# Storing a third of the decoded weights one block later, with a re-timed planner

## The chip, the cores and the metric

The kernel runs on one core of one Trainium2 chip. The metric is the device time of that core in microseconds, from one execution of the whole program. One profiled execution is read besides. Its engines are TensorE (PE, with its weight loads as PEld), VectorE (DVE), ScalarE (ACT), GpSimd (POOL) and SyncE (SP). Each takes its instructions in the order of the program.

## The reference

Attention with a distance bias, then two feed-forward networks (FFNs) on its output. All inputs are fp32 in value; the weights come to the device as 64-bit floats.

```python
B, H, S, D = 4, 8, 576, 64
scores = q @ k.T / sqrt(D)
cum    = cumsum(max(s, 0))
scores = where(causal, -1e9, scores + min(-(cum_i - cum_j), 0))
attn   = softmax(scores) @ v
x = attn reshaped to (2304, 512)
x = ((x @ w_a) * (x @ w_b)) @ w_out              # 512 -> 1536 -> 512
h = x @ w_in                                     # 512 -> 2048
g = max(h, 0) + alpha * min(h, 0)
out = g @ w_out2                                 # 2048 -> 512
```

## The kernel before

**Tiling.** The 2304 tokens are cut into five blocks, here called 1 to 5: four of 512 and one of 256. A block's FFN runs over 12 tiles of 128 hidden features of the first network and 16 of the second. Each product of fp32 numbers is three matmuls of halves that TensorE takes at full rate (fp32r): each factor is split into a high part, the value rounded, and a low part, the rest. `mm3` (L1078 to L1080) issues the three, with the weight's halves `wh` and `wl`; L1189 to L1191 do it for the last layer. A block takes 68 weights of 128x512 numbers (`NW`), and each feeds 4 x 3 = 12 matmuls.

**Where a weight comes from.** In block 1 it is loaded as 64-bit numbers (`raw<-in_w_dram`, 512 KB), then decoded to fp32: `top` on ACT (L987) and `w` on DVE (L278). `split` then makes `wh` on ACT (L270) and `wl` on DVE or POOL (L284). The decoded weight is also stored to a scratch tensor in DRAM, `w_d` (L1051, a DMA that ACT issues). In blocks 2 to 5 two decoded weights are loaded at a time (`raw<-w_d`, 512 KB) and only split. Six buffers hold split weights, five hold `raw`, and a handful hold `w32`, the decoded weight, which in block 1 comes free when the store has landed.

**Other work on the same engines.** In the first network `a_sb` is copied from a PSUM bank by ACT and `g` multiplied by DVE from the other bank; in the second, `m` (ACT, L262, then a scale on DVE, L289) and `g` (DVE). Each `g` is split into `gh` (ACT) and `gl` (DVE or POOL). PE can reuse a bank when its `g` is done. The attention of the next block is cut into steps that PE runs between the FFN's matmuls. Its bias tile `z` is made from `cb`, the cumulated sums broadcast over 128 rows by DMA (`cb<-cum_d`), on ACT (L575) or DVE; the softmax's sums and scales are on ACT, DVE and POOL (`z<-z,sm`, L289); `zt` transposes a tile on DVE, SP stores it (`zd<-zt`) and loads it back transposed (`pt<-zd`). `kh`, `kl` and `qs` are the split keys and queries.

**What sets the order.** The order of ACT, DVE, POOL and SP is made by a planner when the program is built. `Order` keeps open links of chains, each with its engines and an assumed duration; it takes the one that could start first by its own clock, and between equal starts the one due first, its ready time plus a slack (`SL_...`). That clock is pushed on by `run.pe(ns)` behind each piece of PE's work, with PE assumed at 2.4 GHz, and by `run.need(chain)` where PE's next instruction reads what the chain makes. `dma` (L293) gives a transfer's assumed rate and landing. `load_w` (L1006) holds the chains of one weight: loading, decoding, splitting, storing. Block by block the main loop (L1206 on) places the attention steps evenly between the FFN's pieces.

## Time and profile before

| | |
|---|---|
| median of three runs | 1001.83 us |
| the runs | 1000.83 to 1004.99 us |
| the profiled execution's own time | 1007.81 us |
| its span | 1006.0 us |
| busy in the span: PE, DVE, ACT, POOL | 982.2, 682.8, 553.5, 243.2 us |
| granted TensorE clock, mean | 0.993 |
| FFN of blocks 1 to 5 starts at | 56, 283.5, 499.8, 711.8, 904.7 us |

The span is what the trace covers; the time of that execution is 1.8 us longer. The page gives busy time of each engine, and the span in 40 slices of 25.15 us. Behind it the trace can be asked for stretches, for waits of an engine (what it lacked, and for how long), and for single instructions. A matmul's duration reaches beyond the start of the next one, so PE's pace is read from its starts.

### The profile page before, as it was taken

What the parts mean: (1) busy time and instruction counts of PE and PEld (TensorE: products, weight loads), DVE (VectorE), ACT (ScalarE), POOL (GpSimd) and SP (SyncE); (2) the same over time, 40 slices, a digit from 0 to 9 for tenths busy, and PEclk for the clock granted to TensorE, in tenths of its full rate; (3) what the DMA queues carried; (4) which work ended last, traced back from release to release, by engine and by line L of the source; (5) the groups of instructions that cost most, each with busy time, mean ns of one, the idle gap of its engine ahead of it and who ended that gap; (6) DMA issues with size and microseconds to landing.
All of it is one profiled execution on the core that took longest, in us unless ns stands there. A gap on an engine that the chain in (4) does not pass through costs nothing.

```text
span 1006.0 us, 16223 instructions
## 1 busy us (share of the span) xinstructions
PE 982.2 (98%) x5381; PEld 810.7 (81%) x5381; DVE 682.8 (68%) x1590; ACT 553.5 (55%) x1133; POOL 243.2 (24%) x307
## 2 busy tenths in 40 slices
PE   6999999998999999999999999999999999999998
PEld 5667777776888888788888888888888888889997
DVE  7887767885578676876468687964454465546685
ACT  5865656775565455654455446544433354446674
POOL 2121112321232233443132134422010032220032
PEclk9999999998999999999999999999999999999999
DMA  6599999999777758449287766554543424327551
GB/s 188 192 280 346 351 331 345 319 320 317 262 236 247 231 172 263 146 144 275 75 268 242 211 202 205 171 174 145 184 143 93 158 92 130 118 72 237 187 173 59
DMA packets 149156, 208.85 MB, mean 208 GB/s; under 512 B 36112, under 2 KB 80144, under 8 KB 149072
## 3 DMA queue, kind: packets, MB, share of 16 engines
q1 hardware_dynamic: 139280, 189.99, 59.2%
q10 hardware_dynamic: 9792, 17.83, 4.7%
q8 instruction: 42, 0.69, 0.3%
q14 instruction: 42, 0.34, 0.1%
HBM read 164.18 MB, written 43.59 MB: 207 GB/s over the span
## 4 chain that ended last, share of the span: by engine, by line
PE 86%; DMA 7%; DVE 3%; issue 1%; ACT 1%; POOL 1%; ACTq 0%; SPq 0%; POOLq 0%; DVEq 0%
PE bank L1078 20%; PE bank L1079 20%; PE bank L1080 19%; PE bank L1189 6%; PE bank L1190 6%; PE bank L1191 6%; PE bank L766 2%; DMA cb<-cum_d 2%; PE bank L502 2%; DMA raw<-in_w_dram 2%; PE bank L528 1%; PE bank L706 1%; DMA kq<-in_kq_b_dram 1%; PE bank L827 1%; DVE z L278 1%
## 5 line engine op out<-in xcount | busy, mean ns | idle before, releaser
L1078 PE MATMUL bank<-xh,wh 128*128 128x512 f32 (+1 forms) x800 | 299.1, 374 | 2.3 <-DVE g L278 2.3
L1079 PE MATMUL bank<-xl,wh 128*128 128x512 f32 (+1 forms) x800 | 295.1, 369 | 0.0
L1080 PE MATMUL bank<-xh,wl 128*128 128x512 f32 (+1 forms) x800 | 295.1, 369 | 0.0
L270 ACT ACTIVATE wh<-raw 128x512 fp32r<-128x512 f32 x268 | 167.3, 626 | 97.8 <-PE bank L1079 59.5
L284 DVE TENSOR_TENSOR wl<-raw,wh 128x512 fp32r<-128x512 f32 x188 | 131.3, 701 | 95.8 <-ACT wh L270 88.8
L284 POOL TENSOR_TENSOR wl<-raw,wh 128x512 fp32r<-128x512 f32 x84 | 111.0, 1322 | 335.8 <-ACT wh L270 292.4
L1078 PEld LDWEIGHTS bank<-xh,wh 128*128 128x128 f32 x800 | 151.0, 189 | 33.2 <-issue 4.1
L1080 PEld LDWEIGHTS bank<-xh,wl 128*128 128x128 f32 x800 | 151.0, 189 | 25.5
L1079 PEld LDWEIGHTS bank<-xl,wh 128*128 128x128 f32 x800 | 151.2, 189 | 25.0
L270 ACT ACTIVATE gh<-g 128x512 fp32r<-128x512 f32 (+1 forms) x140 | 82.3, 588 | 71.2 <-DVE g L278 68.2
L1189 PE MATMUL bank<-wh,gh 128*128 128x512 f32 x288 | 114.9, 399 | 4.6 <-ACT wh L270 4.6
L284 DVE TENSOR_TENSOR gl<-g,gh 128x512 fp32r<-128x512 f32 (+1 forms) x128 | 87.8, 686 | 43.6 <-ACT gh L270 41.9
L1190 PE MATMUL bank<-wl,gh 128*128 128x512 f32 x288 | 113.5, 394 | 0.0
L1191 PE MATMUL bank<-wh,gl 128*128 128x512 f32 x288 | 112.9, 392 | 0.0
L262 ACT ACTIVATE z<-z,mn 128x128 f32<-128x128 f32 (+4 forms) x144 | 82.9, 577 | 50.8 <-DVE mn L278 50.8
L1078 PE MATMUL bank<-gh,wh 128*128 128x512 f32 (+1 forms) x240 | 89.9, 374 | 1.1 <-ACT wh L270 1.1
L1079 PE MATMUL bank<-gl,wh 128*128 128x512 f32 (+1 forms) x240 | 88.7, 370 | 0.2 <-DVE gl L284 0.2
L1080 PE MATMUL bank<-gh,wl 128*128 128x512 f32 (+1 forms) x240 | 88.5, 369 | 0.0
L262 ACT ACTIVATE m<-bank 128x512 f32<-128x512 f32 (+1 forms) x80 | 44.2, 552 | 75.5 <-PE bank L1080 75.3
L289 DVE TENSOR_SCALAR m<-m,alpha_sb 128x512 f32<-128x512 f32 (+1 forms) x68 | 33.0, 486 | 59.6 <-ACT m L262 58.7
L1189 PEld LDWEIGHTS bank<-wh,gh 128*128 128x128 f32 x288 | 54.8, 190 | 17.6 <-ACT wh L270 5.0
L270 ACT ACTIVATE a_sb<-bank 128x512 f32<-128x512 f32 (+1 forms) x60 | 32.9, 548 | 62.1 <-PE bank L1080 58.3
(91 smaller groups left out, 1369.2 us busy)
## 6 DMA issues: line engine op xcount, KB each, us to landing
raw<-w_d SPq DMA_DIRECT2D x136, 512.0 KB, 4.2
raw<-in_w_dram SPq DMA_DIRECT2D x68, 512.0 KB, 6.0
w_d<-w ACTq DMA_DIRECT2D x68, 256.0 KB, 5.6
zd<-zt SPq DMA_DIRECT2D x48, 192.0 KB, 4.2
pt<-zd SPq DMA_DIRECT2D x48, 192.0 KB, 3.9
kq<-in_kq_a_dram SPq DMA_DIRECT2D x16, 512.0 KB, 5.7
vb<-in_v_dram SPq DMA_DIRECT2D x112, 64.0 KB, 4.0
zd<-zt SPq DMA_DIRECT2D x24, 256.0 KB, 2.2
```

Of the source, the lines that this page charges most:

```text
L262: nc.scalar.activation(o, i, func, **k)
L270: nc.scalar.activation(o, i, AF.Copy, scale=by)
L284: (nc.gpsimd if eng == "pool" else nc.vector).tensor_tensor(o, i0, i1, op=ALU.subtract)
L289: (nc.gpsimd if eng == "pool" else nc.vector).tensor_scalar(o, i, s0, s1, op0=ALU.mult, op1=ALU.mult)
L502: nc.tensor.matmul(d, qs[:, r * P:n], k[:, 0:n], start=i == 0, stop=i == 1)
L766: nc.tensor.matmul(pv[64 * j:64 * j + 64, r * P:(r + 1) * P], got[0][:, c, j * D:(j + 1) * D], p[:, :, r * (r + 1) // 2 + c, :], start=c = ...
L1078: nc.tensor.matmul(o, wh, ih, start=first, stop=False)
L1079: nc.tensor.matmul(o, wh, il, start=False, stop=False)
L1080: nc.tensor.matmul(o, wl, ih, start=False, stop=last)
L1189: nc.tensor.matmul(acc[t], gh[:, c], wh, start=first, stop=False)
L1190: nc.tensor.matmul(acc[t], gh[:, c], wl, start=False, stop=False)
L1191: nc.tensor.matmul(acc[t], gl[:, c], wh, start=False, stop=last)
```

## The change

**A third of the weights.** Pairs of weights with `i // 2 % 3 == 1`, 22 of 68, are not stored in block 1. In block 2 they are loaded as 64-bit numbers again, decoded in place (`w` lies in the first half of `raw`) and stored from there; `raw` comes free when that store has landed. From block 3 on all are loaded as pairs. So block 1 has 46 stores in place of 68 and block 2 has 22 in place of none; `raw<-in_w_dram` goes from 68 to 90, `raw<-w_d` from 136 to 125, `top` and `w` from 68 to 90 each.

**Planner's durations.** PE's matmuls get a gap of 13.3 ns and some attention steps a further 100 or 200 ns; transfers are assumed at 85 (170) bytes per ns, not 90 (180), and land 1500 ns, not 900, behind their end.

**Layer chains first.** The chains on which the FFN itself hangs (`copy_a`, `gate`, `rectify`, the split of `g`, the split of the first network's output) get a slack of -4000 ns, so they come before others that could start at the same time.

**Attention steps by what is ready.** A step whose scores, transposes or values are not ready by the planner's clock may be up to four steps late (`BEHIND`), and where PE would wait for a layer's chain, steps that are ready are placed there, up to four early (`EARLY`).

The core of the diff:

```diff
 BIG = 3.0e38
+GAP, SWITCH, LANDS = 13.3, 100, 1500
...
-SL_LOAD, SL_PARTS, SL_QK, SL_BIAS = 10000.0, 5000.0, 5000.0, 2500.0
+SL_LOAD, SL_PARTS, SL_QK, SL_BIAS, SL_FFN = 10000.0, 5000.0, 5000.0, 2500.0, -4000.0
...
-FASTER, BEFORE = 1.06, 6
+FASTER, BEFORE, BEHIND, EARLY = 1.06, 6, 4, 4
...
-        yield {"dma": prod(o.shape) / (180 if o.dtype == U16 else 90)}, 900
+        yield {"dma": prod(o.shape) / (170 if o.dtype == U16 else 85)}, LANDS
...
         i = n % NW
+        postponed = i // 2 % 3 == 1
+        new = n < NW or (n < 2 * NW and postponed)
+        kept = new and postponed == (n >= NW)
...
-            yield of_w32
-            w = wraw.tile([P, WN], I32, name="w32", tag="w32", bufs=W32)
...
+            if n < NW:
+                yield of_w32
+                w = wraw.tile([P, WN], I32, name="w32", tag="w32", bufs=W32)
...
+            else:
+                w = r[:, 0:WN]
             source.append(w)
             yield from decode(n, r, w)
-            run.give(of_raw, run.t)
+            if n < NW:
+                run.give(of_raw, run.t)
...
-            yield from split(f32(source[0]) if n < NW else source[0], h, l)
-            if n < NW:
+            yield from split(f32(source[0]) if new else source[0], h, l)
+            if kept:
                 run.spawn(keep(stored), run.t)
+            elif new:
+                run.give(of_w32, run.t)
...
-            run.give(of_w32, run.t)
+            run.give(of_w32 if n < NW else of_raw, run.t)
...
-        fetched = run.spawn(first() if n < NW else again(), slack=SL_LOAD)
-        stored = run.spawn(store()) if n < NW else None
+        fetched = run.spawn(first() if new else again(), slack=SL_LOAD)
+        stored = run.spawn(store()) if kept else None
...
-        run.pe(3 * o.shape[-1] / 2.4)
+        run.pe(3 * (o.shape[-1] / 2.4 + GAP))
...
+    def due():
+
+        while todo and want - (steps_in - len(todo)) > 0:
+            run.pump()
+            if want - (steps_in - len(todo)) < BEHIND and not possible(*todo[0]):
+                return
+            step()
+
+    def wait(*chains):
+
+        run.pump()
+        while not seen(*chains) and todo and possible(*todo[0]):
+            if steps_in - len(todo) - want >= EARLY:
+                break
+            step()
+            run.pump()
+        run.need(*chains)
...
-                used[0] = run.spawn(copy_a())
+                used[0] = run.spawn(copy_a(), slack=SL_FFN)
...
-                used[1] = run.spawn(gate(f))
+                used[1] = run.spawn(gate(f), slack=SL_FFN)
```

`possible` asks whether the chains that a step reads are done by the planner's clock; `take`, `into` and the layers call `wait` where they called `run.need`, and the same slack goes to `rectify`, `split_t` and `split_by`.

**What it moves.** All of PE's instructions are the same, and in the same sequence but for attention steps in blocks 2 and 3 that stand one to four units of matmuls away. On the other engines three places matter. The numbers behind names are the builder's and differ between the two kernels.

ACT late in block 1, in the second network. Before, with `wh_2855` the block's weight 57, and `z_2851` the bias made from the second half of `cb`:

```order
L262 ACTIVATE m_2809<-bank3_101 128x512
L270 ACTIVATE gh_2820<-g_2815 128x512
L987 ACTIVATE top1_137<-raw_2648 128x512
L262 ACTIVATE m_2847<-bank2_100 128x512
L987 ACTIVATE top0_136<-raw_2658 128x512
L1051 DMA w_d_135<-w32_2832 128x512
L575 ACTIVATE z_2851<-cb1_2696,cumq_118 128x576
L270 ACTIVATE gh_2868<-g_2861 128x512
L1051 DMA w_d_135<-w32_2842 128x512
L270 ACTIVATE wh_2855<-w32_2832 128x512
L270 ACTIVATE wh_2878<-w32_2842 128x512
```

After, with weights 57, 58 and 59 as `wh_2778`, `wh_2807` and `wh_2837`, and that bias as `z_2835`:

```order
L271 ACTIVATE wh_2778<-w32_2652 128x512
L576 ACTIVATE z_2763<-cb0_2694,cumq_118 128x128
L576 ACTIVATE z_2763<-cb0_2694,cumq_118 128x256
L576 ACTIVATE z_2773<-cb0_2695,cumq_118 128x128
L576 ACTIVATE z_2773<-cb0_2695,cumq_118 128x256
L263 ACTIVATE m_2809<-bank3_101 128x512
L271 ACTIVATE wh_2807<-w32_2708 128x512
L271 ACTIVATE gh_2825<-g_2819 128x512
L271 ACTIVATE wh_2837<-w32_2732 128x512
L576 ACTIVATE z_2835<-cb1_2698,cumq_118 128x576
L263 ACTIVATE m_2864<-bank2_100 128x512
L988 ACTIVATE top0_136<-raw_2718 128x512
```

The splits of weights 57 and 58, which stood behind the bias and behind two stores, now stand ahead of it, and that of 59 with them.

DVE late in block 2, in the second network. Before, `g_4679` is a layer's `g`, `m_4632` its scaled part, `z_4466` and `z_4467` the scores of two heads:

```order
L284 TENSOR_TENSOR qs_4604<-kq_4317,qs_4604 64x512
L278 RECIPROCAL sm_4610<-sm_4610 128x1
L278 TENSOR_SCALAR sm_4612<-sm_4612 128x1
L278 RECIPROCAL sm_4612<-sm_4612 128x1
L289 TENSOR_SCALAR z_4466<-z_4466,sm_4610 128x512
L289 TENSOR_SCALAR z_4467<-z_4467,sm_4612 128x512
L289 TENSOR_SCALAR m_4632<-m_4632,alpha_sb_97 128x512
L284 TENSOR_TENSOR qs_4607<-kq_4318,qs_4607 64x512
L289 TENSOR_SCALAR m_4663<-m_4663,alpha_sb_97 128x512
L278 STREAM_TRANSPOSE zt_4669<-z_4466 128x512
L278 STREAM_TRANSPOSE zt_4676<-z_4467 128x512
L278 SCALAR_TENSOR_TENSOR g_4679<-bank3_101,m_4632 128x512
```

After, the same `g` is `g_4685`, the next one `g_4725`, and the scores of the first head `z_4499`:

```order
L285 TENSOR_TENSOR kl_4644<-kq_4351,kh_4642 128x512
L290 TENSOR_SCALAR m_4672<-m_4672,alpha_sb_97 128x512
L285 TENSOR_TENSOR qs_4643<-kq_4351,qs_4643 64x512
L279 SCALAR_TENSOR_TENSOR g_4685<-bank3_101,m_4672 128x512
L279 TENSOR_SCALAR sm_4649<-sm_4649 128x1
L279 TENSOR_SCALAR sm_4651<-sm_4651 128x1
L279 RECIPROCAL sm_4649<-sm_4649 128x1
L279 RECIPROCAL sm_4651<-sm_4651 128x1
L285 TENSOR_TENSOR gl_4695<-g_4685,gh_4694 128x512
L290 TENSOR_SCALAR m_4710<-m_4710,alpha_sb_97 128x512
L290 TENSOR_SCALAR z_4499<-z_4499,sm_4649 128x512
L279 SCALAR_TENSOR_TENSOR g_4725<-bank2_100,m_4710 128x512
```

The layer's `m` and `g` have moved ahead of the softmax's sums, scales and transposes; both transposes now come behind the second `g`.

ACT early in block 2, in the first network. Before, `wh_3588` and `wh_3612` are the halves of one pair:

```order
L270 ACTIVATE wh_3541<-raw_3337 128x512
L270 ACTIVATE kh_3571<-kq_3374 128x512
L270 ACTIVATE kh_3574<-kq_3375 128x512
L270 ACTIVATE qs_3572<-kq_3374 128x512
L270 ACTIVATE a_sb_3590<-bank2_100 128x512
L262 ACTIVATE z_3519,sm_3578<-z_3519,mn_3577 128x512
L262 ACTIVATE z_3520,sm_3580<-z_3520,mn_3579 128x512
L270 ACTIVATE wh_3588<-raw_3413 128x512
L270 ACTIVATE wh_3612<-raw_3413 128x512
L270 ACTIVATE gh_3625<-g_3615 128x512
L270 ACTIVATE wh_3650<-raw_3479 128x512
```

After, the same two weights are `wh_3586` and `wh_3610`, decoded from `raw_3408` and `raw_3440`:

```order
L1061 DMA w_d_135<-raw_3408 128x512
L988 ACTIVATE top1_137<-raw_3440 128x512
L271 ACTIVATE kh_3569<-kq_3367 128x512
L271 ACTIVATE a_sb_3588<-bank2_100 128x512
L271 ACTIVATE kh_3572<-kq_3368 128x512
L263 ACTIVATE z_3520,sm_3576<-z_3520,mn_3575 128x512
L263 ACTIVATE z_3521,sm_3578<-z_3521,mn_3577 128x512
L1061 DMA w_d_135<-raw_3440 128x512
L271 ACTIVATE qs_3573<-kq_3368 128x512
L271 ACTIVATE gh_3621<-g_3613 128x512
L271 ACTIVATE wh_3586<-raw_3408 128x512
L271 ACTIVATE wh_3610<-raw_3440 128x512
```

Two stores from `raw` and a decoding `top` have come in ahead of the splits of this pair.

## Rows read from the trace of the kernel before

**Rows 1.** The page: span, DMA busy tenths and GB/s in 40 equal slices.

```profile
span 1006.0 us, 16223 instructions
...
DMA  6599999999777758449287766554543424327551
GB/s 188 192 280 346 351 331 345 319 320 317 262 236 247 231 172 263 146 144 275 75 268 242 211 202 205 171 174 145 184 143 93 158 92 130 118 72 237 187 173 59
```

**Rows 2.** Stages: window, length, busy us by engine, PEclk, DMA share, GB/s.

```profile
56.00:283.50 227.50, 220.82 (x1175) 174.41 (x1174) 170.77 (x384) 146.88 (x285) 46.55 (x56) 0.98 0.93 312
283.50:499.80 216.30, 213.98 (x1137) 177.40 (x1136) 154.88 (x365) 114.04 (x241) 73.31 (x93) 0.99 0.64 201
```

**Rows 3.** What PE waited for: us in total, times, longest us.

```profile
PE bank L1189 <- ACT wh L270: 4.6, 1, 4.6
PE bank L1078 <- DVE g L278: 2.3, 1, 2.3
PE bank L733 <- DVE z L289: 2.0, 1, 2.0
...
PE bank L1078 <- ACT wh L270: 1.1, 1, 1.1
```

**Rows 4.** Timeline of PE around 247 us: start us, duration us, engine, line, operation.

```profile
240.06 0.39 PE L1078 MATMUL bank<-xh,wh 128*128 128x512 f32 x1
...
242.55 0.39 PE L1080 MATMUL bank<-xh,wl 128*128 128x512 f32 x1
...
251.08 0.63 PE L1190 MATMUL bank<-wl,gh 128*128 128x512 f32 x1
251.51 0.63 PE L1191 MATMUL bank<-wh,gl 128*128 128x512 f32 x1
...
253.10 0.39 PE L1078 MATMUL bank<-xh,wh 128*128 128x512 f32 x1
```

**Rows 5.** Timeline of SP and of ACT before it; brackets hold the wait ahead.

```profile
237.25 0.49 SPq L295 DMA_DIRECT2D cb<-cum_d  x1
...
245.68 0.77 ACT L575 ACTIVATE z<-cb,cumq 128x576 f32<-128x576 f32 x1 [5.28 <-DMA cb<-cum_d]
```

**Rows 6.** Timeline of PE and ACT from 156 to 159 us.

```profile
156.22 0.39 PE L1080 MATMUL bank<-xh,wl 128*128 128x512 f32 x1
156.67 0.33 ACTq L1051 DMA_DIRECT2D w_d<-w  x1
...
157.04 1.15 ACT L270 ACTIVATE wh<-w 128x512 fp32r<-128x512 f32 x2 [1.68 <-DMA cb<-cum_d]
...
158.78 0.40 PE L1078 MATMUL bank<-gh,wh 128*128 128x512 f32 x1
```

**Rows 7.** Timeline of PE, then of DVE, around 412 us.

```profile
409.30 0.39 PE L1191 MATMUL bank<-wh,gl 128*128 128x512 f32 x1
...
417.14 0.39 PE L1189 MATMUL bank<-wh,gh 128*128 128x512 f32 x1
...
405.71 0.69 DVE L284 TENSOR_TENSOR qs<-kq,qs 64x512 fp32r<-64x512 f32 x1
...
410.09 1.29 DVE L278 STREAM_TRANSPOSE zt<-z 128x512 f32<-128x512 f32 x2
411.31 1.24 DVE L278 SCALAR_TENSOR_TENSOR g<-bank,m 128x512 f32<-128x512 f32 x2
```

**Rows 8.** By line or tile: engine, operation, count: ns min/median/max, first, last start.

```profile
L987 ACT ACTIVATE top<-raw x68: 757/780/804, 37.0 to 276.5; 128x512 f16<-128x512 bf16 x68
...
L278 DVE SCALAR_TENSOR_TENSOR w<-raw,top x68: 641/684/1267, 37.8 to 277.4; 128x512 int32<-128x512 int32 x68
...
L289 DVE TENSOR_SCALAR z<-z,sm x100: 269/486/1626, 20.4 to 861.3; 128x512 f32<-128x512 f32 x29, 128x384 f32<-128x384 f32 x26, 128x128 f32<-128x128 f32 x17, 128x576 f32<-128x576 f32 x16
```

**Rows 9.** The page, DMA issues: engine, count, KB each, median us to landing.

```profile
raw<-w_d SPq DMA_DIRECT2D x136, 512.0 KB, 4.2
raw<-in_w_dram SPq DMA_DIRECT2D x68, 512.0 KB, 6.0
```

More of the change, by code (lines that the diff above doesn't have):

```diff
@@ L504, in q_k @@
                     )
-            run.pe(4 * (n / 2.4 + 13))
+            run.pe(4 * (n / 2.4 + GAP))
             if r == 3:
@@ L525, in q_k @@
                         )
-            run.pe(2 * n / 2.4)
+            run.pe(2 * n / 2.4 + 2 * SWITCH)
         for j, o in enumerate(own):
@@ L530, in q_k @@
             )
-        run.pe(4 * n / 2.4)
+        run.pe(4 * n / 2.4 + 2 * SWITCH * (r > 1))
         if r == 3:
@@ L837, in av_b @@
                 )
-        run.pe(5 * 107)
+        run.pe(5 * 107 + 4 * SWITCH)
         run.give(of_vb)
@@ L1021, in first @@
             yield from dma(r.bitcast(U16)[:, 1:1 + 4 * WN], w64[i].bitcast(U16))
-            yield of_w32
-            w = wraw.tile([P, WN], I32, name="w32", tag="w32", bufs=W32)
-            if n == NW - 1:
-                for j in range(2):
-                    run.give(of_stack, run.t)
+            if n < NW:
+                yield of_w32
+                w = wraw.tile([P, WN], I32, name="w32", tag="w32", bufs=W32)
+                if n == NW - 1:
+                    for j in range(2):
+                        run.give(of_stack, run.t)
+            else:
+                w = r[:, 0:WN]
             source.append(w)
             yield from decode(n, r, w)
-            run.give(of_raw, run.t)
+            if n < NW:
+                run.give(of_raw, run.t)
         def again():
@@ L1051, in store @@
             nc.scalar.dma_start(w_d[i].bitcast(I32), source[0])
-            yield {"dma": P * WN / 90}, 900
+            yield {"dma": P * WN / 85}, LANDS
         def keep(stored):
             yield stored
-            run.give(of_w32, run.t)
+            run.give(of_w32 if n < NW else of_raw, run.t)
         source = []
-        fetched = run.spawn(first() if n < NW else again(), slack=SL_LOAD)
-        stored = run.spawn(store()) if n < NW else None
+        fetched = run.spawn(first() if new else again(), slack=SL_LOAD)
+        stored = run.spawn(store()) if kept else None
         turns[n] = run.spawn(acquire())
@@ L1072, in take @@
         got, ready = loaded[taken - 1]
-        run.need(ready)
+        wait(ready)
         return got
@@ L1080, in mm3, with seen, possible, step @@
         nc.tensor.matmul(o, wl, ih, start=False, stop=last)
-        run.pe(3 * o.shape[-1] / 2.4)
+        run.pe(3 * (o.shape[-1] / 2.4 + GAP))
     o_done = {}
+    todo, want = [], 0
+    def seen(*chains):
+        return all(c.done and c.time <= run.now + 100 for c in chains)
+    def possible(f, args):
+        rings = 1 if f == two_av else 2
+        if f not in (s01, s23, s4, two_av):
+            return True
+        if not seen(*(reader[i] for i in ring[:rings] if i in reader)):
+            return False
+        if f == two_av:
+            a, b, hp, _ = args
+            keys = [(a, 2 * hp + j, r) for j in range(2) for r in (0, 2, 3)] + [(b, hp, 4)]
+            return all(k in e_t and seen(e_t[k]) for k in keys) and seen(
+                v_t[a, hp, 0][1], v_t[b, hp, 1][1]
+            )
+        b, hp = args[:2]
+        if f == s4:
+            return seen(kq_t[b, hp, 1][1], z_t[b, hp, 4][1])
+        r = args[2] if f == s23 else 0
+        return seen(kq_t[b, hp, 0][1], *(z_t[b, 2 * hp + j, r][1] for j in range(2)))
+    def step():
+        f, args = todo.pop(0)
+        f(*args)
+    def due():
[12 more added lines that the diff above has]
+        run.need(*chains)
     def ffn(blk):
@@ L1093, in into @@
             if j in used:
-                run.need(used[j])
+                wait(used[j])
             for k in range(KD):
                 if k in x2:
-                    run.need(x2[k])
+                    wait(x2[k])
                 c = slice(k * P, (k + 1) * P)
@@ L1111, in split_g @@
             gl = gp.tile([P, T], F32R, name="gl", tag="gl")
-            g_done[f] = gh, gl, run.spawn(split_t(g, gh, gl), run.t)
+            g_done[f] = gh, gl, run.spawn(split_t(g, gh, gl), run.t, SL_FFN)
         def copy_a():
@@ L1155, in ffn @@
                 yield from into(0)
-                used[0] = run.spawn(copy_a())
+                used[0] = run.spawn(copy_a(), slack=SL_FFN)
                 yield from into(1)
-                run.need(used[0])
-                used[1] = run.spawn(gate(f))
+                wait(used[0])
+                used[1] = run.spawn(gate(f), slack=SL_FFN)
             if f >= 1:
@@ L1162, in ffn @@
                 gh, gl, ready = g_done.pop(f - 1)
-                run.need(ready)
+                wait(ready)
                 for d in range(KD):
@@ L1171, in ffn @@
                         x2[d] = run.spawn(
-                            split_by(o, xhb[:, d, 0:T], xlb[:, d, 0:T], SHRUNK ** 2)
+                            split_by(o, xhb[:, d, 0:T], xlb[:, d, 0:T], SHRUNK ** 2), slack=SL_FFN
                         )
@@ L1180, in ffn @@
                 yield from into(f % 2)
-                used[f % 2] = run.spawn(rectify(f, ab[f % 2][:, 0:T]))
+                used[f % 2] = run.spawn(rectify(f, ab[f % 2][:, 0:T]), slack=SL_FFN)
             if f >= 2:
@@ L1184, in ffn @@
                 gh, gl, ready = g_done.pop(f - 2)
-                run.need(ready)
+                wait(ready)
                 first, last = f == 2, f == NF2 + 1
@@ L1191, in ffn @@
                     nc.tensor.matmul(acc[t], gl[:, c], wh, start=False, stop=last)
-                    run.pe(3 * 213)
+                    run.pe(3 * (213 + GAP))
                     if last:
@@ L1220, in attention_two_moe_kernel @@
         total = NF1 * 3 * KD + NF2 * (KD + T // P)
-        done = 0
+        todo[:], steps_in, want = steps, len(steps), 0
         for i, _ in enumerate(ffn(blk)):
-            want = min(len(steps), (i + 1) * len(steps) * FASTER / total)
-            while done < want:
-                f, args = steps[done]
-                f(*args)
-                done += 1
-        assert done == len(steps)
+            want = min(steps_in, (i + 1) * steps_in * FASTER / total)
+            due()
+        while todo:
+            step()
     while run.open:
```

## The prediction, made before the changed kernel ran

> **What bounds the kernel now.** I read the page first: a span of 1006.0 us, the engines in 40 slices, DMA busy to nine tenths and more in slices 3 to 10 [rows 1]. Then the stages, cut where TensorE (PE) starts each FFN block: in block 1 (56 to 283.5 us) DMA is at 0.93 and 312 GB/s, in block 2 (283.5 to 499.8 us) at 0.64 and 201 GB/s, and in both PE is idle for a few us only [rows 2]. So PE sets the time, and what can be won is what PE waits. Its list of waits names it: after the first 60 us there are three that count, 4.6 and 1.1 us for a split weight (`wh`, ScalarE) and 2.3 us for a gate (`g`, VectorE) [rows 3]. The rest of the list is small or lies in the first 60 us.
>
> A wait costs more than its idle time, since PE's first matmuls behind it are slow. So I price each by PE's starts. In an undisturbed stretch 11 starts take 242.55 - 240.06 = 2.49 us, 0.2264 us each [rows 4].
>
> *Stall B, 7.6 us.* From the start at 242.55 to the one at 253.10 there are 13 steps in 10.55 us; at the pace they take 2.94, so 7.61 are lost [rows 4]. Of these 4.6 are the wait; the rest is that the clock came back at its lower level, 1.2 GHz: the starts at 251.08 and 251.51 are 0.43 us apart [rows 4]. The cause: SP issued the second half of `cb` at 237.25, it landed 8.4 us later, and ScalarE (ACT), in order, stood for 5.28 us before the `z` that reads it [rows 5]. The weight that PE wanted was queued behind that `z`.
>
> *Stall A, 1.65 us.* From 156.22 to 158.78 there are 4 steps in 2.56 us; the pace gives 0.91 [rows 6]. Here ACT stood before a store of a weight (`w_d<-w`, issued by ACT), which the trace puts down to the landing of another `cb`; the split of the next two weights was behind it [rows 6].
>
> *Stall C, 4.2 us.* From 409.30 to 417.14 there are 16 steps in 7.84 us; the pace gives 3.62, so 4.22 are lost [rows 7]. No DMA is in it: VectorE (DVE) ran a scale and two transposes of attention's before the `g` that frees PE's bank [rows 7].
>
> Together 1.65 + 7.61 + 4.22 = 13.48 us.
>
> **The change, part by part.**
>
> *PE's order.* It is the same instructions in the same sequence but for some attention steps of blocks 2 and 3 that move by one to four units of matmuls. Removed and added work on PE: none. I cost it at nothing; a late step would show as a wait on PE, and is part of the third rival.
>
> *Weights ahead, in block 1.* I counted, at the 28 places in block 1 where ACT first reads a layer's bank, how many weights ACT has split beyond the one PE has just used: before 1 to 4, mean 2.9; now 5 or 6, mean 5.2 (six buffers hold split weights). In the later blocks it is about 5 in both. One weight is 12 matmuls, 12 x 0.2264 = 2.72 us, so PE gets 2.3 x 2.72 = 6.3 us more cover against anything that holds ACT. The reason is the 22 weights that are not stored in block 1: their buffer comes free after the split, not after a landing, and ACT issues 46 stores there, not 68.
>
> *Stall B.* The `z` of B now stands behind three more splits; the weight that PE lacked (the block's number 57) is split before the four biases ahead of it. The last split ahead of `z` takes the buffer of weight 53, so PE has done 53 by then and can run 54 to 57, 4 x 2.72 = 10.9 us, before it needs a bank that the `m` behind `z` must empty; scale and gate behind that `m` take some 2 us. 9 us of cover stand against 5.28 us of waiting, or 8.4 us if ACT came at the moment of the issue [rows 5]. So B goes whole, -7.61.
>
> *Stall A.* The same cover of 5 weights stands against 1.68 us [rows 6]. -1.65.
>
> *Stall C.* `g` now stands right behind the first `qs`; two scales, a second `qs`, an `m` and both transposes come after it. In the trace that `qs` was done by 406.4 and `g` began at 411.31, so it can be nearly 5 us earlier, and PE wants it at 409.53 [rows 7]. -4.22. What is late next are the transposes and the `pt` loads behind them, for a step that PE reaches tens of us later; SP's store of the transposed tile waits for them, with the loads of weights behind it on SP, which run further ahead than that (below).
>
> *Decoding again in block 2.* 22 more `top` on ACT at 0.780 are 17.2 us, 22 more `w` on DVE at 0.684 are 15.0 us [rows 8]. Block 2 lasts 216.3 us with DVE busy 154.9 and ACT 114.0 [rows 2]: they lie in 61 and 102 us of idle time. If that cover is gone, each costs PE its own length. Between nothing and 15.0 us I take nothing, since 169.9 of 216.3 is 0.79, near block 1's share of 0.75, where no wait of PE's was for a full DVE.
>
> *Traffic.* Block 1 loses 22 stores of 256 KB, 5.8 MB of some 312 x 227.5 = 71 MB. Block 2 gains those 5.8 MB, and 11 more loads of 512 KB, since a raw weight takes what a pair of decoded ones took: 43.5 + 11.5 = 55 MB in 216.3 us, 254 GB/s against block 1's 312 [rows 2]. A load of raw weights landed in 6.0 us, one of decoded ones in 4.2 [rows 9]; five `raw` buffers now hold seven weights or so, 7 x 2.72 = 19 us ahead. I take nothing for block 2, and nothing for shorter landings in block 1, where the cover alone is enough.
>
> A rule of the Trainium skill speaks against this part. The row shows 351 GB/s in the busiest slice [rows 1]. Perfetto Trace Analysis, § Roofline, puts one core's ceiling at its 16 DMA engines' 435 GB/s. By that, 351 is no ceiling, and fewer bytes would shorten no landing: by the rows as by the rule my sum is the same as long as the cover is enough, and rival 1's if it is not. No run here shows more than 351, so the trace does not bear the rule out.
>
> *ACT's queue in block 2.* 22 stores that were not there; 15 of them also wait for an older DMA. Behind each stand `wh` and `gh`, and PE behind those. Bounds by the nearest rows: nothing, or A's 1.65 to B's 7.61 each; I take nothing, since 5 weights are split ahead (13.6 us).
>
> *DVE and POOL.* Eleven scales of `z` go from POOL to DVE, 0.486 us each, 5.3 us in all [rows 8]; they lie in idle time.
>
> *First 60 us.* ACT and DVE run the first softmax tiles in another order. The 2.0 us for a scaled `z` [rows 3] may go, or as much may be added, since the following loads free no earlier. I take 0 and keep +-2.
>
> **Sum.** 1007.81 (the profiled execution: 1006.0 of span and 1.8 around it) - 13.48 = 994.3; I say 994. The runs shown have a median of 1001.83, 6.0 below the profiled one. If these 6 us lie in the stalls, which hang on when transfers land (the three runs differ by 4.2 among themselves), the floor is common and 994 holds for unprofiled runs too. If they lie everywhere, it is 988.4. I take the first: PE's pace is the clock's.
>
> **Rivals.**
>
> 1. *Landings still hold PE.* The 16 DMA engines stay nearly full in block 1 (65 of 71 MB), ACT is held longer than the cover, and only C, which is order alone, goes: 1001.83 - 4.22 = 997.6, up to 1001.8 if another gate takes C's place. For it: DMA at 0.93. Against it: 5 weights of cover. The rule of Perfetto Trace Analysis named above, from the Trainium skill, would lead here.
>
> 2. *The floor is lower in unprofiled runs*: 988.4, as above.
>
> 3. *Block 2 becomes what block 1 was; slower.* A store stands in ACT's queue before `wh` until an older transfer has landed, at DVE 0.79 the decode it also waits for is late, and `raw` buffers come free only after the store. One such event as large as B costs 7.61; two take the gain away: 994.3 + 15.2 = 1009.5. For it: block 2 had C already. Against it: 254 GB/s, and as many weights split ahead there as before. One event alone gives 1002, no difference. The point from which it decides is the second.
>
> **How the numbers follow.** Forecast 0.60, rival 1 0.20, rival 2 0.13, rival 3 0.07. Faster by over 0.5% (below 996.8; 0.5% is about what a measurement of this kernel can tell from no change): the forecast but for 0.03, rival 2, and 0.04 of rival 1, 0.74. Within 0.5%: 0.03 and 0.16 of rival 1, 0.19. Slower: 0.07. The range reaches down to rival 2 and up over most of rival 1: 988 to 1001.
>
> **What would show it.** Right: PE's list of waits has no `wh` and no `g` over 0.5 us after 60 us, the granted clock is 1.00 in every slice after the first, and the span is some 13 us shorter, all of it before 420 us. B wrong: ACT waits for `cb` and PE for `wh` near 245. C wrong: PE waits for `g` near 410. Rival 3: PE waits for `wh` between 283 and 500, behind a store on ACT's queue. The traffic is right if the rate of block 1 falls below 300 GB/s and that of block 2 rises to some 250.

## The result and the profile after

The changed kernel takes 1014.64 us (median of four runs, 1013.58 to 1019.25), the kernel before 1003.41 in the same comparison: a ratio of 1.0116, 95% interval 1.0089 to 1.0143. It is slower by 1.2%, where 994 us and a gain had been forecast; the time lies outside the range.

The profiled execution took 1013.68 us with a span of 1011.8, against 1007.81 and 1006.0 before. So the two traces differ by 5.8 us and the medians by 11.2: the one before was 4.4 above its median, the one after 1.0 below. The traces explain the direction and about half of the size; no pair of traces contains the rest. Part of it may lie in the kernel before: of its 28 executions beside e14 to e16 (below), the 14 with a mean granted clock of 0.997 have a median of 1001.7 us, and the 5 with 0.993, which the profiled one also had, of 1007.1. PE came back from stall B at its lower clock, so a lower mean clock points to longer stalls, and to less that could be won in a typical execution than in the profiled one. No run shows that directly.

The page of the changed kernel (span, engines, DMA and rate in 40 slices), against [rows 1]:

```profile
span 1011.8 us, 16294 instructions
...
PE 982.5 (97%) x5381; PEld 809.1 (80%) x5381; DVE 704.5 (70%) x1628; ACT 563.2 (56%) x1152; POOL 239.0 (24%) x294
...
DMA  7689999797868998678386757454542534327551
GB/s 180 222 276 337 292 317 304 266 301 262 267 212 293 292 267 295 212 244 266 111 271 219 238 181 235 156 186 145 181 135 83 168 93 137 112 71 240 188 173 57
```

PE's work is the same (982.5 us for 982.2): what the change costs is again what PE waits. The two stages with the decoding, in the columns of [rows 2]:

```profile
56.00:283.50 227.50, 216.40 (x1146) 170.07 (x1147) 165.84 (x374) 138.81 (x273) 46.67 (x53) 0.98 0.88 288
283.50:499.80 216.30, 213.14 (x1136) 175.99 (x1137) 175.76 (x397) 126.59 (x262) 69.02 (x86) 1.00 0.78 251
```

The traffic has moved as worked out: 312 to 288 GB/s in the first window, 201 to 251 in the second. But PE is busy for 4.4 us less in the first window, where it was to gain. Its list of waits (total, times, longest), against [rows 3]:

```profile
PE bank L1088 <- DVE g L279: 5.9, 3, 3.3
...
PE bank L519 <- DVE mn L279: 3.3, 4, 1.6
PE bank L1088 <- ACT gh L271: 3.2, 1, 3.2
PE bank L1243 <- ACT gh L271: 1.7, 1, 1.7
PE bank L503 <- DVE mn L279: 1.2, 2, 0.6
```

No `wh` is left in it: that half of the forecast held. In its place stand `g`, `gh` and attention's row maxima `mn`. The FFN matmuls come in the same sequence in both kernels, so the start of the k-th in one can be set against the k-th in the other; the steps of this difference say where time went:

| place (us in the trace after) | what | us |
|---|---|---|
| start of block 1 | begins at 53.6, not 56.0 | -2.4 |
| A, B, C | gone, as forecast | -1.7, -7.5, -5.2 |
| D, 69 | PE waits for `g` | +5.0 |
| E, 182 | PE waits for `gh` | +4.9 |
| F, 257 and 264 | PE waits for `g`, twice | +3.1 |
| G, 284 and 289 | PE waits for `gl`, `gh` | +3.1 |
| H, 428 | PE waits for `mn`, an attention step | +2.6 |
| others, under 1.6 each | mostly attention steps | +3.7 |
| sum | | +5.6 |

So 14.4 us were won (13.5 forecast) and 2.4 at the start, and 22.4 were lost at new places, most of it in block 1, which ends at 291.8 us in this trace. What stands behind E, F and D can be read in three timelines. E first: ACT, then DVE, then PE (brackets hold the wait ahead and what ended it):

```profile
169.70 0.79 ACT L988 ACTIVATE top<-raw 128x512 f16<-128x512 bf16 x1 [0.85 <-DMA raw<-in_w_dram]
...
173.23 0.79 ACT L988 ACTIVATE top<-raw 128x512 f16<-128x512 bf16 x1 [2.17 <-DMA raw<-in_w_dram]
...
177.03 0.79 ACT L988 ACTIVATE top<-raw 128x512 f16<-128x512 bf16 x1 [2.54 <-DMA raw<-in_w_dram]
177.69 0.57 ACT L271 ACTIVATE a_sb<-bank 128x512 f32<-128x512 f32 x1
...
181.22 0.63 ACT L271 ACTIVATE gh<-g 128x512 fp32r<-128x512 f32 x1 [1.04 <-DVE g L279]
...
178.99 0.15 DVE L279 TENSOR_SCALAR sm<-sm 128x1 f32<-128x1 f32 x1 [0.44 <-ACT z L263]
...
180.53 0.65 DVE L279 TENSOR_TENSOR g<-bank,a_sb 128x512 f32<-128x512 f32 x1
...
178.29 0.39 PE L1090 MATMUL bank<-gh,wl 128*128 128x512 f32 x1
181.90 0.79 PE L1088 MATMUL bank<-gh,wh 128*128 128x512 f32 x1 [3.22 <-ACT gh L271]
```

Three times in 8 us ACT stood before a `top` until its raw weight had landed, 5.6 us in all. The `a_sb` of the layer was queued behind the third. On DVE a softmax sum that waited for ACT's `z`, a scale and a transpose stood ahead of `g`, which began 2.3 us after `a_sb` was done, at 180.53; `gh` came at 181.22, and PE had stood for 3.22 us. It was not a weight that was late.

F, SP's load of the bias rows, ACT and PE:

```profile
247.39 0.61 SPq L296 DMA_DIRECT2D cb<-cum_d  x1
...
254.51 0.78 ACT L576 ACTIVATE z<-cb,cumq 128x576 f32<-128x576 f32 x1 [8.22 <-DMA cb<-cum_d]
...
257.07 0.50 PE L1088 MATMUL bank<-xh,wh 128*128 128x512 f32 x1 [1.86 <-DVE g L279]
```

ACT reached the `z` of stall B a microsecond before its `cb` was even issued, since SP was late, and stood for 8.22 us; `m` and `g` behind it were late for PE. (In SP's list of waits between 240 and 246 us, 4.6 us are for the landing of a store `w_d<-w`.)

D, DVE and PE:

```profile
66.29 0.58 DVE L279 STREAM_TRANSPOSE zt<-z 128x384 f32<-128x384 f32 x1 [3.49 <-DMA zd<-zt]
...
68.52 0.68 DVE L279 TENSOR_TENSOR g<-bank,a_sb 128x512 f32<-128x512 f32 x1
...
69.25 0.79 PE L1088 MATMUL bank<-xh,wh 128*128 128x512 f32 x1 [3.26 <-DVE g L279]
```

DVE stood 3.49 us before a transpose whose target buffer was still being stored, with the `g` behind it.

All three are one pattern: an engine stands, in order, for a transfer, and behind it in its queue is something with little cover. The longer of the two waits of G is not: there DVE ran a `qs` and the low half of a weight ahead of the `m` and the `g`, without standing for any transfer (DVE, then PE):

```profile
284.38 0.69 DVE L285 TENSOR_TENSOR qs<-kq,qs 64x512 fp32r<-64x512 f32 x1
285.10 1.73 DVE L285 TENSOR_TENSOR wl<-raw,wh 128x512 fp32r<-128x512 f32 x1
286.75 0.47 DVE L290 TENSOR_SCALAR m<-m,alpha_sb 128x512 f32<-128x512 f32 x1
287.25 0.69 DVE L279 SCALAR_TENSOR_TENSOR g<-bank,m 128x512 f32<-128x512 f32 x1
...
288.66 0.50 PE L1243 MATMUL bank<-wh,gh 128*128 128x512 f32 x1 [1.70 <-ACT gh L271]
```

How much more ACT stood is in its list of waits between 56 and 500 us, the raw weights' line of the kernel after and then of the kernel before:

```profile
ACT top L988 <- DMA raw<-in_w_dram: 30.5, 21, 3.4
...
ACT top L987 <- DMA raw<-in_w_dram: 5.9, 5, 2.0
```

The transfers are not slower: a raw load in block 1 lands 5.8 us after its issue (median), 6.0 before (DMA issues between 56 and 283.5 us, after, then before: count, KB each, median us to landing).

```profile
raw<-in_w_dram SPq DMA_DIRECT2D x60, 512.0 KB, 5.8
...
raw<-in_w_dram SPq DMA_DIRECT2D x58, 512.0 KB, 6.0
```

But `top` now stands closer behind its load. Paired weight by weight in block 1, the median time from a load's issue to the start of its `top` is 7.6 us, and was 11.0.

### The profile page after: what moved, and what is told of

Its sections match the earlier page's. It is cut to its first block, busy times and chain, and to the rows that moved or that the text cites. A ratio compares the mean times of both kernels' runs of the same rounds, so it can differ in the third digit from the quotient of the medians.

```text
span 1011.8 us, 16294 instructions
## 1 busy us (share of the span) xinstructions
PE 982.5 (97%) x5381; PEld 809.1 (80%) x5381; DVE 704.5 (70%) x1628; ACT 563.2 (56%) x1152; POOL 239.0 (24%) x294
## 4 chain that ended last, share of the span: by engine, by line
PE 80%; DVE 8%; DMA 7%; ACT 3%; issue 2%; ACTq 0%; SPq 0%; POOL 0%; DVEq 0%; POOLq 0%
PE bank L1088 19%; PE bank L1089 19%; PE bank L1090 18%; PE bank L1243 5%; PE bank L1245 5%; PE bank L1244 5%; DMA raw<-in_w_dram 2%; PE bank L767 2%; DMA cb<-cum_d 2%; PE bank L503 2%; DVE z L279 1%; PE bank L707 1%; PE bank L828 1%; PE bank L529 1%; DVE w L279 1%
## 5 line engine op out<-in xcount | busy, mean ns | idle before, releaser
L285 DVE TENSOR_TENSOR gl<-g,gh 128x512 fp32r<-128x512 f32 (+1 forms) x132 | 92.5, 701 | 46.1 <-ACT gh L271 44.0
L988 ACT ACTIVATE top<-raw 128x512 f16<-128x512 bf16 x90 | 69.8, 786 | 35.7 <-DMA raw<-in_w_dram 30.5
L290 DVE TENSOR_SCALAR m<-m,alpha_sb 128x512 f32<-128x512 f32 (+1 forms) x72 | 36.9, 512 | 52.5 <-ACT m L263 51.4
L285 POOL TENSOR_TENSOR wl<-w,wh 128x512 fp32r<-128x512 f32 x28 | 37.8, 1350 | 136.5 <-ACT wh L271 83.8
```

The lines of the kernel that those rows point to most:

```text
L285: (nc.gpsimd if eng == "pool" else nc.vector).tensor_tensor(o, i0, i1, op=ALU.subtract)
L290: (nc.gpsimd if eng == "pool" else nc.vector).tensor_scalar(o, i, s0, s1, op0=ALU.mult, op1=ALU.mult)
L988: nc.scalar.activation(top.bitcast(F16).rearrange("p (n t) -> p n t", t=2)[:, :, 1], r.bitcast(BF16)[:, 4:4 + 4 * WN].rearrange("p (n t) - ...
```

## The experiments

All are built from the changed kernel unless said otherwise. "Waits" is ACT's line for `top` and raw weights between 56 and 500 us (us, times); "distance" the median from a raw load's issue to its `top` in block 1. Ratios are to the kernel before, run on the same chip beside each.

| kernel | median us | ratio (95%) | waits | distance |
|---|---|---|---|---|
| before | 1003.4 | 1 | 5.9, 5 | 11.0 |
| after | 1014.6 | 1.0116 (1.0089 to 1.0143) | 30.5, 21 | 7.6 |
| e1 all stored early | 1001.3 | 0.9983 (0.9965 to 1.0001) | 6.2, 7 | 10.0 |
| e2 postponed only | 1002.6 | 0.9987 (0.9968 to 1.0007) | 32.8, 21 | 9.0 |
| e3 no layer first | 1018.3 | 1.0149 (1.0115 to 1.0183) | 37.6, 26 | 7.2 |
| e4 old durations | 1006.1 | 1.0032 (1.0005 to 1.0059) | 21.1, 16 | 9.0 |
| e6 raw lands later | 1006.5 | 1.0033 (1.0016 to 1.0049) | 0.3, 1 | 10.3 |
| e7 all land later | 1003.6 | 1.0014 (0.9994 to 1.0034) | 17.7, 13 | 8.4 |
| e8 early, all later | 1008.3 | 1.0066 (1.0042 to 1.0089) | none | 11.1 |
| e9 buffer back later | 1014.3 | 1.0112 (1.0083 to 1.0141) | 33.7, 18 | 7.8 |
| e10 later past start | 1005.1 | 1.0006 (0.9987 to 1.0026) | 23.0, 15 | 8.3 |
| e11 raw 7000 | 998.9 | 0.9946 (0.9925 to 0.9967) | 10.6, 8 | 9.9 |
| e12 postponed only, raw later | 1003.6 | 0.9990 (0.9973 to 1.0007) | 3.9, 3 | 10.0 |
| e13 early, raw sooner | 1009.9 | 1.0058 (1.0039 to 1.0077) | 20.7, 18 | 8.4 |
| e14 early, raw 7000 | 1003.1 | 0.9992 (0.9973 to 1.0011) | none | 12.7 |
| e15 raw 5500 | 999.0 | 0.9955 (0.9934 to 0.9976) | 15.0, 11 | 8.8 |
| e16 raw 8500 | 998.5 | 0.9943 (0.9920 to 0.9965) | 1.6, 2 | 10.9 |
| e17 store planned | 1006.3 | 1.0035 (1.0013 to 1.0057) | 10.2, 8 | 10.7 |
| e19 store planned, later | 1000.4 | 0.9955 (0.9935 to 0.9975) | none | 11.8 |

**One part alone.** First the change was taken apart.

```diff
-        postponed = i // 2 % 3 == 1
+        postponed = False
```

> The changed kernel with all 68 weights stored in block 1, as in the kernel before; the planner's new durations, layer chains first and placing of steps stay. Theory 1, the postponed storing brings the new waits (ACT stands before top for raw weights 30.5 us in all, 5.9 before): they go, the gains at 157, 247 and 412 us stay, 990 to 997 us, ratio to before 0.987 to 0.994. Theory 2, the new order brings them: 1008 to 1018 us, ratio 1.005 to 1.015, with PE waiting for g or gh for 3 us or more in block 1 again.

1001.3 us: neither. E is not there and A, B and C are gone, but D stays (4.9 us lost between 59 and 70 us). Set matmul by matmul against the changed kernel, whose trace ends 12.7 us behind it, e1 is 12.8 us ahead when block 2 begins: the whole difference arises in block 1. Block 2 takes 213.8 us in e1 and 213.6 in the changed kernel, which decodes 22 weights in it.

e2 is the kernel before with the change's lines in `load_w` alone, and none in the planner:

> The kernel before with the postponed storing alone: old durations, no layer chains first, steps placed evenly. Theory 1 (the postponed storing brings the new waits): 1008 to 1016 us, ACT waits for raw weights for 20 us or more. Theory 2 (the new order brings them): 992 to 1003 us, since 22 stores fewer in block 1 shorten the landing that held ACT at 247 us, and ACT waits for raw weights for under 12 us.

1002.6 us, the time of theory 2, but with 32.8 us of waits, as in theory 1. So these waits need not cost PE much: it is their place that counts. Neither half alone is slower than the kernel before; the loss is in the two together.

```diff
-SL_LOAD, SL_PARTS, SL_QK, SL_BIAS, SL_FFN = 10000.0, 5000.0, 5000.0, 2500.0, -4000.0
+SL_LOAD, SL_PARTS, SL_QK, SL_BIAS, SL_FFN = 10000.0, 5000.0, 5000.0, 2500.0, 0.0
```

> The changed kernel with the slack of the layer chains at 0 instead of -4000. If layer chains first is what puts top, z and zt (which wait for transfers) ahead of others at the wrong time: 998 to 1006 us and no wait of PE for g at 69 us. If not, 1010 to 1018 us as the changed kernel, and the wait for g at 412 us (4.2 us with its slow clock) may come back on top.

1018.3 us, and PE waited 7.2 us for `g`: layer chains first is not the cause. (The fourth part, attention steps by what is ready, was not taken out by itself.)

```diff
-GAP, SWITCH, LANDS = 13.3, 100, 1500
+GAP, SWITCH, LANDS = 0.0, 0, 900
...
-        yield {"dma": prod(o.shape) / (170 if o.dtype == U16 else 85)}, LANDS
+        yield {"dma": prod(o.shape) / (180 if o.dtype == U16 else 90)}, LANDS
```

(and 90 for 85 in the store)

> The changed kernel with the old durations in the planner: no gap per matmul, no extra for attention steps, transfers at 90 (180) bytes per ns that land 900 ns later. If the waits come from transfers that land later than the planner assumes: more of them, ACT waits for raw weights for over 30 us and the time is 1015 to 1030 us. If the durations do nothing: 1010 to 1018 us. If the new durations are what made the order worse: 995 to 1005 us.

1006.1 us: not the first case, and nearest the third. With the old durations the distance is greater (9.0 us) and block 1 ends 15.1 us earlier in the trace: D, F, G and half of E are gone. A new wait of attention's at 324 us takes 6.7 us back. So the new durations made this order worse in block 1; which of them did is not shown.

**The distance itself.** Now the place of `top` was moved by one number.

```diff
-        yield {"dma": prod(o.shape) / (170 if o.dtype == U16 else 85)}, LANDS
+        yield {"dma": prod(o.shape) / (170 if o.dtype == U16 else 85)}, LANDS + 3000 * (o.dtype == U16)
```

(only the raw loads are of type U16)

> The changed kernel with one number of the planner's changed: a load of raw weights is assumed to land 3 us later (4500 ns for 1500), so that top is put further behind its load. In the traces so far the median time from a raw load's issue to its top in block 1 is 11.0 us before the change, 7.6 after it, 10.0 with all weights stored early and 9.0 with the postponed storing alone, against a landing of 5.8 to 6.0 us. Theory 3, the postponed storing gives buffers back sooner, so the order lets top follow its load so soon that ACT stands for the landing and a_sb and gh behind it are late: the median goes to 9.5 us or more, ACT's waits for raw weights fall from 30.5 to under 12 us, the wait for gh at 182 us (5 us lost) goes, 1004 to 1009 us, ratio 1.000 to 1.006. Rival, the traffic moved to block 2 or the stores there cost the time: no change, 1012 to 1018 us.

All as theory 3 had it: 1006.5 us, distance 10.3, and of the waits of `top` for raw weights this is what is left:

```profile
DMA raw<-in_w_dram: 0.3, 1
```

E is all but gone. D is not, and it shows that the same pattern stands on DVE too (DVE, then PE):

```profile
67.43 0.58 DVE L279 STREAM_TRANSPOSE zt<-z 128x384 f32<-128x384 f32 x1 [4.48 <-DMA zd<-zt]
...
70.62 0.80 PE L1088 MATMUL bank<-xh,wh 128*128 128x512 f32 x1 [4.24 <-DVE g L279]
```

The opposite edit, without any postponed storing (`postponed = False`, and `LANDS - 3000` for the raw loads):

> The opposite edit: the changed planner with all weights stored in block 1 (1001.3 us, ACT waited 6.2 us for raw weights, 10.0 us from issue to top), and raw weights assumed to land 3 us sooner. If the place of top behind its load is what costs, and not the postponed storing as such: the median from issue to top falls to 8.5 us or less, ACT waits 20 us or more for raw weights, 1005 to 1013 us. Rival, the buffers and not the assumed landing place top where all weights are stored early: the median stays at 9.5 us or more and the time at 999 to 1003 us.

1009.9 us, distance 8.4, waits 20.7: a loss of this size can be had without postponing anything, though at other places (3.2 us at 172 us, 2.5 about 258, 1.7 at 285, against e1). Within each of the two pairs the bytes are the same and the time moved with one assumed landing. The whole order moves with that number, so this doesn't show that the distance by itself sets the time.

**All transfers.** `LANDS` at 4500, first with the postponed storing, then without:

> The changed kernel with every transfer assumed to land 3 us later (4500 ns for 1500), so besides raw weights also the bias rows (cb), for which ACT stood 8.2 us at 254 us, and the transposed tiles (zd), for which DVE stood 3.5 us before the g that PE wants at 69 us. Theory 3, widened to all transfers: the losses at 69 us (5.0), 182 us (5.1) and 257 to 264 us (3.0) go, 998 to 1004 us. Rival, the new losses are the order's own and not the landings': 1010 to 1018 us.

> The changed planner with all weights stored in block 1 (1001.3 us, ratio 0.998) and every transfer assumed to land 3 us later. Theory 3: the 4.9 us lost between 59 and 70 us there go, 994 to 998 us, ratio 0.990 to 0.995, faster than both kernels. Rival: the loss at 69 us is the order's own and stays, 999 to 1004 us.

1003.6 and 1008.3 us. D, E and F are gone in e7, but for some 1 us at D, and from the start of block 1 on it gains 11.1 us on the kernel before. But block 1 begins at 62.5 us, since PE waits at the start for the first keys and queries (waits of PE in e7):

```profile
PE bank L529 <- DMA kq<-in_kq_a_dram: 8.1, 2, 4.6
```

The same start costs e8 its gain, 8.4 us against e1. Without it e8 would be at some 1000 us (an estimate from the two starts of block 1, 62.4 and 54.1), still not in theory 3's range: D is down to 1.4 us, but a wait for `gh` at 282 us is new, 4.2 us. So 4500 was then used from block 1 on only (`run.lands`, set to `LANDS + 3000` ahead of the loop over the blocks):

> The changed kernel with transfers assumed to land after 4500 ns, but only from the start of block 1 on; in the first part, up to some 55 us, 1500 ns stay. With 4500 ns everywhere the kernel took 1003.6 us: its block 1 began 8.9 us later than the changed kernel's (62.5 for 53.6 us), and from there on it won 11.1 us on the kernel before. Theory 3 (the order lets readers follow their loads too soon; the loss in the first part is a loss of its own): the two add up, block 1 begins at 53 to 55 us and the time is 993 to 997 us, ratio 0.989 to 0.994, faster than both kernels. Rival, a late start merely gives the loads a lead that hides landings: the waits for g and gh in block 1 come back, 1001 to 1008 us.

The rival: 1005.1 us. Block 1 begins at 53.3, but with the late start gone the waits for raw weights grow from 17.7 to 23.0 us, and E is back (ACT, then PE):

```profile
179.17 0.78 ACT L989 ACTIVATE top<-raw 128x512 f16<-128x512 bf16 x1 [2.08 <-DMA raw<-in_w_dram]
179.82 0.60 ACT L272 ACTIVATE gh<-g 128x512 fp32r<-128x512 f32 x1
...
180.47 0.79 PE L1089 MATMUL bank<-gh,wh 128*128 128x512 f32 x1 [2.97 <-ACT gh L272]
```

e11 puts raw weights 2500 ns later still, e15 1000, e16 4000:

> As the last one, with raw weights assumed 2.5 us later still (7000 ns). Theory 3: ACT's waits for raw weights, 17.7 us where all landed at 4500 ns and 0.3 us where only raw weights did, fall under 8 us; since those that are left cost PE nothing there, the time is that of the last one within 2 us, 992 to 998 us. Rival (a late start gives the lead): 1000 to 1008 us.

> The same kernel with the postponed storing, raw weights assumed to land after 5500 ns instead of 7000 (at 4500 it took 1005.1 us with 23.0 us of waits for raw weights, at 7000 it took 998.9 with 10.6). Theory 3: in between, waits of 11 to 20 us and 999 to 1004 us. Rival (each order is a draw, and the waits for raw weights are not what decides): any time from 998 to 1010 us, without regard to the waits.

> The same with 8500 ns. Theory 3: waits for raw weights under 8 us and 997 to 1001 us, since there is little left to win. Rival (each order is a draw): any time from 998 to 1010 us. If decoding then comes too late for the weights: PE waits for wh, over 1003 us.

998.9, 999.0 and 998.5 us: all three are faster than the kernel before by 0.5%, and than the changed one by some 1.6%. The first lies just outside both of its ranges, and its waits, 10.6 us, are not under 8; the other two lie in the ranges of theory 3 and of the draw alike, so these two times do not tell them apart. From 5500 to 8500 ns the time is flat while the waits fall from 15.0 to 1.6 us. So the time does not follow the sum of the waits. At 4500 one of them still falls right ahead of the `gh` of E, which PE needs; at 5500 the nearest one lies 2 us ahead of its `a_sb`, and 0.9 us of the wait for `gh` is left. PE's list of e15, whose profiled execution took 994.88 us at a granted clock of 1.00:

```profile
PE bank L520 <- DVE mn L280: 2.4, 3, 1.7
...
PE bank L1089 <- ACT gh L272: 0.9, 1, 0.9
```

On top of e2 the later raw weights were tried too (3900 ns for 900):

> The kernel before with the postponed storing alone (1002.6 us, ACT waited 32.8 us for raw weights), and in the planner raw weights land 3 us later (3900 ns for 900). Theory 3: the waits for raw weights fall under 10 us, the 4 us that were lost at 113 and 177 us go, 996 to 1000 us, ratio 0.992 to 0.997. Rival, the postponed storing costs by its traffic: 1001 to 1005 us.

Waits down to 3.9 us as expected, the time not: 1003.6. It loses at D (5.4 us near 70 us, with DVE before `zt`), which raw weights don't touch.

**What the postponed storing does by itself.** e14 is e11 with `postponed = False`:

> The kernel that took 998.9 us (landings assumed 4500 ns from block 1 on, raw weights 7000 ns), with all weights stored in block 1. If the postponed storing gains something once top stands far enough behind its load: slower than 998.9, 1001 to 1005 us. If the gain is the order's alone: within 2 us of it, 997 to 1001 us.

1003.1 us, 4 more than e11, and the intervals of the two ratios do not meet: with these landings the kernel with the postponed storing is the faster one. Between the two traces some 4.6 us are lost about 250 to 270 us, where ACT stands for a store again and PE for a weight, as in stall B, and 3.3 us at D, where DVE stands for a transposed tile and no weight's store plays a part. So not all of the 4 us is the storing's own (ACT's list, then PE's):

```profile
ACT wh L272 <- DMA w_d<-w: 5.7, 2, 5.2
...
PE bank L1089 <- ACT wh L272: 2.8, 1, 2.8
```

e17 lets the planner count the 22 stores of block 1 that are not made:

```diff
-            nc.scalar.dma_start(w_d[i].bitcast(I32), source[0])
+            if kept:
+                nc.scalar.dma_start(w_d[i].bitcast(I32), source[0])
...
-        stored = run.spawn(store()) if kept else None
+        stored = run.spawn(store()) if new else None
```

> The changed kernel, but the planner still counts the time of the 22 stores in block 1 that are not made (its 330 ns of ACT and 771 ns of transfer each); none of them is issued. In the program the instructions of ACT other than stores, and the loads of SP, then stand in block 1 in the same order as with all weights stored early (1001.3 us, 10.0 us from issue to top, 6.2 us of waits for raw weights), and only the traffic differs. Theory 3 (order): the median from issue to top is 10 us or more, ACT waits under 8 us for raw weights, 996 to 1002 us, so the postponed storing in itself costs nothing or gains a little. Rival, the postponed storing costs in itself (loads and stores in block 2, fewer stores in block 1): 1008 to 1016 us.

1006.3 us, between the two. The distance is back (10.7), and with e1's order in block 1 the trace stays within 2 us of e1's there. So the order moved because the planner no longer counted the stores' own time: the buffers come free as early in e17 as in the changed kernel. That is 8.4 of the 13.3 us between e1 and the changed kernel by the medians, and 11.3 of the 12.8 us that the changed kernel's trace loses on e1's up to the start of block 2. In block 2 e17 loses 3.6 us on e1, though the changed kernel lost nothing there, and 2.6 of them at one place, the H of the table above (PE, then DVE in e17):

```profile
419.37 0.33 PE L503 MATMUL bank<-kh,qs 128*128 128x128 f32 x1 [1.97 <-DVE mn L279]
420.35 0.47 PE L503 MATMUL bank<-kh,qs 128*128 128x128 f32 x1 [0.54 <-DVE mn L279]
...
417.65 1.28 DVE L285 TENSOR_TENSOR wl<-raw,wh 128x512 fp32r<-128x512 f32 x2
...
419.23 0.69 DVE L279 SCALAR_TENSOR_TENSOR raw<-raw,top 128x512 int32<-128x512 int32 x1
```

A decoding and two low halves stand on DVE around the row maxima that PE's attention step waits for. The low halves stand there in e1 too, which decodes nothing in block 2, and PE waits once in place of twice:

```profile
415.62 0.33 PE L503 MATMUL bank<-kh,qs 128*128 128x128 f32 x1 [1.38 <-DVE mn L279]
```

> The last kernel with every transfer assumed to land after 4500 ns from block 1 on. Theory 3: what the last one still loses to the landing of a transposed tile near 69 us goes too: 994 to 999 us. Rival, a new order brings other waits of its own: 1000 to 1006 us.

1000.4 us, just in the rival's range: no wait for raw weights is left, but PE waits for `g` at 71 us for 4.3 us, so D stays in this order, and the longer landing alone does not remove it.

The buffers were put to the test directly in e9: the changed kernel, whose planner gives the buffer of a postponed weight back 5 us after its split, about when a store would have. By theory 3 as it first stood, with the buffers at its root, the distance was to go back to 9.5 us or more and the time to 1001 to 1008 us. It took 1014.3 us, with a distance of 7.8 and 33.7 us of waits. Its output is wrong, so its time is a hint only, but it points where e17 does: not to the buffers.

Over all kernels of the table, the three with a distance under 8 us are the slowest, 1014.3 to 1018.3 us. From 8.3 us on there is no order in it: 8.8 goes with 999.0 and 11.1 with 1008.3. So a short distance is a warning; what a new order costs beyond that was not foretold by any of these numbers, and for single times the rival "each order is a draw" stays open.

## Why the prediction was wrong, point by point

- **Stalls A, B, C.** Right: forecast -1.65, -7.61 and -4.22, measured -1.7, -7.5 and -5.2. B came back in part as F (3.1): I gave 9 us of cover against 8.4 at most, out of 10.9 us that PE could run and some 2 us from `m` to `g`. ACT stood 8.2; with 0.7 for `z` itself, which I had left out, and 1.9 from `m` to PE that makes 10.8 us, and PE ran on for 8.9, not 10.9.
- **Weights ahead.** The step that failed. The count was right (PE never waits for `wh`), but I wrote that PE gets "6.3 us more cover against anything that holds ACT". The cover of five weights is a cover of weights only. `a_sb` and `gh` stand in the same queue, and PE wants them two or three weights later, 5.4 to 8.2 us, whatever lies in the buffers; at the end of the first network, where no further tile comes between, one weight later, 2.7 us. E (4.9) stands there: its piece is the last of that network. E and F are 8.0 of the 22.4 us lost; D, G and H are DVE's, to whose new order the sum gave no price.
- **Traffic.** The rates came out as worked out (254 forecast, 251 measured in block 2). What I did not look at is the distance between a load and its reader, which the change shortened from 11.0 to 7.6 us. Landings hardly got shorter with 24 GB/s less (5.8 us for 6.0), and the busiest slice is 337 GB/s. The Trainium skill's Perfetto Trace Analysis, § Roofline, puts one core's ceiling at some 435 GB/s. No slice of any run here is over 359, so the ceiling itself is not tested; what I had drawn from it, that fewer bytes shorten no landing, holds to 0.2 us.
- **First 60 us.** I took 0 within 2 us. Block 1 began 2.4 us earlier, but D behind it cost 5.0; only PE's own waits up to 56 us had been looked at, not the queues that reach across.
- **Decoding in block 2.** I took nothing between 0 and 15.0 us, and that held: block 2 takes 213.6 us in the changed kernel, with DVE at 0.81 (forecast 0.79), and 213.8 in e1, which decodes nothing there. H (2.6) is no loss against e1, which has 2.8 at that place. e17 shows that it can be more in another order, 3.6 us, through DVE and not through the stores: ACT stood for no store in block 2.
- **Rivals and chances.** The third rival had the right kind of event, an engine held in order for a transfer, but in block 2 and with a chance of 0.07; the loss came in block 1. I priced the stalls that the trace showed and gave the new order, which differs on ACT and DVE in nearly every stretch, no price of its own.
- **Profile and median.** I took the 6 us above the median for part of the stalls, which fits the clocks of the executions, and left 994 for typical executions as well. Of the medians' difference about half is not in the two traces.

What stays open is how the rest of the 11.2 us is shared out in unprofiled executions, and what D hangs on: it is there with and without the postponed storing, is small in e7 and e10, and stays in e14 and e19, which assume the same landing of its transfers. The time also doesn't follow one number: e2 and e15 have long waits that cost little, so that only the place of each wait, read in the timeline, tells its price.

## What to carry to other kernels

In a hand-planned order, price a change by the distance between each load and the first instruction that stands for it, on every in-order queue, and by what is queued right behind; more data ready ahead covers only those who read that data. When work is taken out of a planner's model (here the stores' time), everything behind it moves up towards the landings, so here the assumed landing had to grow with it. Where a new order removes known stalls, expect new ones of like size until the places behind each transfer have been looked through.

## What the runs showed of the hardware

Fewer stores did not spare SP the waits for them. Between 56 and 500 us SP stood 14.6 us for landings of block 1's stores, which ACT issues, before the change, and 28.8 us after it, though there are 22 stores fewer; the `cb` of F is a load that came late behind such a wait (SP's lists, before, then after):

```profile
SPq L295 <- DMA w_d<-w: 14.6, 11, 4.4
...
SPq L296 <- DMA w_d<-w: 28.8, 12, 5.3
```

And a landing hardly depends on the rate here: raw loads in block 1 took a median of 5.4 to 6.0 us in ten traces that were compared, 5.8 at 288 GB/s and 6.0 at 316, with the shortest, 5.4, at 299 and 305.
